# Taking a feed-forward network's two layers in turns on TensorE, product by product, from the seventeenth step on

## The chip, the cores and the metric

One core of a Trainium2 chip. The metric is the device time of one execution in microseconds; lower is better.

## The reference

A chunked attention with memory tokens feeds a squared-ReLU feed-forward network. Cut to what matters:

```python
# attention: 4 batches x 8 heads x 768 positions x 64; chunks of 32 queries,
# each sees 16 positions to the left, 8 to the right and 8 memory tokens (64 keys)
for c in range(nc):
    scores = scale * np.matmul(q_c, k_full.transpose(0, 1, 3, 2))
    scores = scores - np.max(scores, axis=-1, keepdims=True)
    a = np.exp(scores)
    a = a / (np.sum(a, axis=-1, keepdims=True) + 1e-09)
    out[:, :, c_start:c_end] = np.matmul(a, v_full)
x = attn_out.transpose(0, 2, 1, 3).reshape(3072, 512)
h = x @ w_in                      # 512 -> 2048
r = np.maximum(h, 0.0)
g = s * (r * r) + b
return (g @ w_out).astype(np.float32)   # 2048 -> 512
```

## The kernel before, in words

The 3072 tokens are cut into 8 chunks of 384 (`TOK`), the 2048 hidden features into 16 blocks of 128. A **step** `u` is one feature block of one chunk; there are 128 (`STEPS`). Each step has two halves on TensorE:

- `hidden(u)`, the first layer: a 128x384 tile `h` in one PSUM bank, summed over 4 blocks of the 512 inputs. Values are split into a high and a low fp32r part, so each block takes three products (high weight with low x, low weight with high x, high with high). That makes 12 matmuls of 384 columns; the weights stand in the array (`w` or `ww`) and `x` streams.
- `result(u)`, the second layer: three 128x512 accumulators (`acc`, one for each 128 tokens, each with its bank), again three products each: 9 matmuls of 512 columns; here the tile `g` stands in the array and the weights stream.

Each matmul has a weight load of its own, which runs beside the matmul ahead of it. Between the halves of a step ScalarE makes relu, square, `s*x+b` and the high part `gH` out of `h`, all in place in PSUM up to the last, and VectorE makes the low part `gL`. There are three `g` tiles and at most two `h` tiles.

The whole program is laid out ahead of time by `Plan`: every operation is put down with its engine, an assumed duration (`HOLD`), its dependences and a priority. `Plan.lay` then runs through time and gives each free engine the ready operation with the lowest priority number; the instructions are written in that order, and the engines work through their queues in it. `hidden(u)` has priority `u` and is put down in pieces (before: 4 pieces of three products); `result(u)` has priority `u + LAG - 0.1` with `LAG = 2`, in three pieces, one for each accumulator. So in the steady part TensorE takes result(u-1), hidden(u+1), result(u), hidden(u+2) and so on, each whole.

Between these lie, every eight steps, the **attention blocks** of the coming chunks: 96 small matmuls for values (line 502) and 96 for scores (line 481) in one pinned chain, then softmax and 24 32x32 transposes on VectorE (line 440). Until about 126 us VectorE and ScalarE also turn the float64 weights into split parts (lines 588 to 597). Names in the profile: `ps` is any PSUM bank, `xH`/`xL` the parts of x, `w`/`ww` prepared weights, `gH`/`gL` the parts of g. Line 610 is the first layer's matmul, 633 the second's.

Of the kernel before, what the change touches and what calls it, by code (L numbers as in the profile page):

```python
# [21 lines left out]
B, H, S, D = 4, 8, 768, 64  # L22
# [3 lines left out]
P = 128  # L26
# [3 lines left out]
NC_T = DM // P  # L30
NF = DFF // P
TOK = 384
# [10 lines left out]
NTURN = 2  # L43
SECOND = 1.0
LAG = 2
NALONE = 2
JOIN = 2.0
APART = 6.0
# [16 lines left out]
def G_AT(i, a):  # L65
# [11 lines left out]
LATE_F = NF - NEARLY  # L77


HOLD = dict(hidden=523, result=690, scores=560, value1=670, value2=670, scores1=540, scores2=540, turn=84, value=1300, wrest=1000, warm=215,  # L80
            relu=388, square=388, affine=565, high=388, xhigh=388, wscale=566, whigh=527, copy=270, exp8=570, exp4=385, keep=480, store=480,
            low=555, rec=90, edge=90, max8=600, max4=335, sub8=600, sub4=335, sum8=600, sum4=335, flip=317, xlow=500, wlow=350, wjoin=640, wsign=617, out=620,
            small=235, norm8=1040, norm4=560, issue=440)
LATE = dict(PE=185, ACT=135, DVE=140, POOL=60, SP=0)
# [6 lines left out]


class Op:
    __slots__ = ("eng", "hold", "fn", "deps", "outs", "prio", "lock", "vals", "n", "start", "end", "left", "ready", "size", "done", "next")


class Val:
# [37 lines left out]
        self.live[v.kind] -= 1  # L135


class Plan:


# [3 lines left out]
    def op(self, eng, kind, prio, fn, reads=(), writes=(), lock=False, size=0):  # L144
        o = Op()
        o.eng, o.hold, o.fn, o.prio, o.lock, o.n, o.size = eng, HOLD[kind], fn, prio, lock, len(self.ops), size
        o.deps, o.outs, o.vals, o.next = set(), [], [], None
        for part in reads:
            o.deps.update(part[1])
        for part in writes:  # L150
            o.deps.update(part[1])
            o.deps.update(part[2])
        for part in reads:
            part[2].append(o)
        for part in writes:
            part[1][:] = [o]
            part[2].clear()
        o.vals = list({id(p[0]): p[0] for p in (*reads, *writes)}.values())
        for v in o.vals:
            v.left += 1  # L160
        self.ops.append(o)
        return o

    def lay(self, filler=None):

# [18 lines left out]
        while todo:  # L184
            t = heapq.heappop(events)
            while events and events[0] <= t:
                heapq.heappop(events)
            while back and back[0][0] <= t:
                v = heapq.heappop(back)[-1]
                v.ring.back(v)  # L190
            for e in engines:
                while waiting[e] and waiting[e][0][0] <= t:
                    o = heapq.heappop(waiting[e])[2]
                    heapq.heappush(ready[e], (o.prio, o.n, o))
                if free[e] > t:
                    continue
                if e == "SP":
                    flying = [x for x in flying if x > t]
                    if len(flying) >= FLIGHT:
                        heapq.heappush(events, min(flying))  # L200
                        continue
                put, got = [], None

                soon = min(((y[2].prio, y[1], y[0]) for y in waiting[e] if y[0] <= t + SOON[e]), default=None) if SOON[e] else None
                while ready[e]:
                    x = heapq.heappop(ready[e])
                    o = x[2]
                    if soon and soon[:2] < x[:2]:
                        put.append(x)
                        heapq.heappush(events, soon[2])  # L210
                        break
                    if e in pin and pin[e] is not o:
                        put.append(x)
                        continue
                    new = [v for v in o.vals if v.slot is None and v.ring.tiles is not None]
                    other = "POOL" if e == "DVE" else "DVE"
                    held = o.lock and e in lock and lock[other] > t

                    if o.lock and e in lock and free[other] <= t and any(y[2].lock and y[:2] < x[:2] for y in ready[other]):
# [24 lines left out]
                o = got  # L244
                o.start = t
# [5 lines left out]
                if o.size:  # L251
                    wire = max(wire, t) + o.size / (RATE if sent >= NSLOW else SLOW)
                    sent += 1
                    o.end = wire + LAND
                    flying.append(o.end)
                if o.lock and e in lock:
                    lock[e] = free[e]
                laid.append((t, o.n, o.fn))
                todo -= 1
                heapq.heappush(events, free[e])  # L260
                for d in o.outs:
                    d.left -= 1
                    d.ready = max(d.ready, free[e] + AGAIN[e] if d.eng == e and not o.size else o.end)
                    if not d.left:
                        heapq.heappush(waiting[d.eng], (d.ready, d.n, d))
                        heapq.heappush(events, d.ready)
                for v in o.vals:
                    v.left -= 1
                    v.done = max(getattr(v, "done", 0.0), o.end)
                    if not v.left and v.ring.tiles is not None:  # L270
                        heapq.heappush(back, (v.done, o.n, o.vals.index(v), v))
                        heapq.heappush(events, v.done)
# [9 lines left out]
def body(ctx: ExitStack, tc: tile.TileContext, qkv, w1, w2, out):  # L282
    nc = tc.nc
# [120 lines left out]
    def xt(x, a, c):  # L404
        return x.tile[2 * a + c // 2][:, c % 2 * TOK:(c % 2 + 1) * TOK]
# [194 lines left out]

    g_vals, h_vals, a_vals, partial = {}, {}, {}, {}

    def hidden(u):
        ch, f = STEPS[u]
        h = Val(ps, "h")
        x, w = x_vals[ch], c_w[0, f]

        def products(c):
            for n, (wi, xi) in enumerate(((0, 1), (1, 0), (0, 0))):
                nc.tensor.matmul(h.tile[:, :TOK], weight_tile(0, f)[:, wi, c * P:(c + 1) * P], xt(x, xi, c), start=(c == 0 and n == 0),  # L610
                                 stop=(c == NC_T - 1 and n == 2))
# [13 lines left out]
    def result(u):  # L625
# [2 lines left out]
        first = u == 0 or STEPS[u - 1][0] != ch  # L628
        last = u + 1 == len(STEPS) or STEPS[u + 1][0] != ch

        def products(acc, t):
            for n, (gi, wi) in enumerate(((1, 0), (0, 1), (0, 0))):
                nc.tensor.matmul(acc.tile, g.tile[gi][:, t * P:(t + 1) * P], weight_tile(1, f)[:, wi, :], start=(first and n == 0), stop=(last and n == 2))  # L633
# [85 lines left out]
```

## Time and profile before

| | |
|---|---|
| median of 3 runs | 627.71 us (625.8, 627.71, 628.86) |
| the profiled execution's own time | 625.31 us |
| its span, from the first to the last instruction | 623.5 us |
| TensorE busy | 97% of the span |
| VectorE and ScalarE busy | 55% each |
| TensorE's granted clock, mean | 0.996 |

The views that follow are of that profiled execution. A matmul's busy time in them (0.34 us for 384 columns, 0.39 us for 512) includes the tail that the next one overlaps; what a matmul costs in a row of matmuls is the distance from its start to the next one's start.

### The profile page before, as it was taken

To read this page: it belongs to the slowest core of one execution; us is meant where nothing else is said; L and a number is where in the kernel's file an instruction comes from. 1 tells how busy PE (TensorE), PEld (TensorE's weight loads), DVE (VectorE), ACT (ScalarE), POOL (GpSimd) and SP (SyncE) were. 2 spreads that over 40 slices of the span, in tenths; PEclk is the share of its full clock that TensorE was granted. 3 is DMA by queue.
4 is the path that set the end of the run, shared out by engine and by line. 5 is a ranking of instruction groups with operands and counts; after the bars stand their busy time and mean duration, and the time that the engine had idled before them with its cause. 6 is when DMAs were issued, how large, how long until landed. Compare 5 with 4: busy or idle time off the path is not lost.

```text
span 623.5 us, 13759 instructions
## 1 busy us (share of the span) xinstructions
PE 605.3 (97%) x5854; PEld 532.3 (85%) x5861; DVE 341.3 (55%) x816; ACT 343.7 (55%) x660; POOL 37.2 (6%) x46
## 2 busy tenths in 40 slices
PE   8898999999999999999999999999999999999997
PEld 5667888888989898898988899898988989899996
DVE  6899999884565462825538182654618355131112
ACT  3577888854555554454455555545555445545543
POOL 2112000000010000101001010100101000000000
PEclk9899999999999999999999999999999999999999
DMA  9944766413041300303022030312103110010001
GB/s 348 400 159 145 243 188 183 131 50 129 1 128 50 112 18 12 134 34 128 1 82 98 2 128 1 129 50 77 53 2 127 52 53 0 2 50 2 1 0 52
DMA packets 17342, 55.42 MB, mean 89 GB/s; under 512 B 1920, under 2 KB 1920, under 8 KB 17280
## 3 DMA queue, kind: packets, MB, share of 16 engines
q1 hardware_dynamic: 17280, 54.53, 25.4%
q8 instruction: 46, 0.75, 0.5%
q14 instruction: 16, 0.13, 0.1%
HBM read 48.24 MB, written 6.29 MB: 87 GB/s over the span
## 4 chain that ended last, share of the span: by engine, by line
PE 82%; DVE 11%; DMA 4%; issue 2%; ACT 1%; POOL 0%; DVEq 0%; SPq 0%; ACTq 0%
PE ps L610 37%; PE ps L633 37%; DMA words<-w 4%; PE ps L502 3%; PE ps L481 3%; DVE wv L591 2%; DVE wv L593 2%; PE ps L371 1%; DVE top L419 1%; DVE t L420 1%; DVE den L422 1%; DVE gL L622 1%; DVE w L597 1%; DVE ww L597 1%; DVE words L589 1%
## 5 line engine op out<-in xcount | busy, mean ns | idle before, releaser
L622 DVE TENSOR_TENSOR gL<-ps,gH 128x384 fp32r<-128x384 f32 x128 | 70.9, 555 | 232.1 <-ACT gH L621 231.2
L618 ACT ACTIVATE ps<-ps 128x384 f32<-128x384 f32 x128 | 60.8, 475 | 191.5 <-PE ps L610 190.5
L610 PE MATMUL ps<-xH,w 128*128 128x384 f32 x512 | 130.9, 336 | 0.3 <-DVE w L597 0.3
L610 PE MATMUL ps<-xH,ww 128*128 128x384 f32 x512 | 130.7, 336 | 0.0
L633 PE MATMUL ps<-w,gH 128*128 128x512 f32 x384 | 119.1, 391 | 0.0
L633 PE MATMUL ps<-ww,gH 128*128 128x512 f32 x384 | 119.0, 391 | 0.0
L610 PEld LDWEIGHTS ps<-xH,w 128*128 128x128 f32 x512 | 92.7, 188 | 3.0 <-DVE w L597 0.9
L610 PEld LDWEIGHTS ps<-xH,ww 128*128 128x128 f32 x512 | 92.8, 188 | 2.2
L440 DVE STREAM_TRANSPOSE aT<-t 32x128 f32<-32x128 f32 x288 | 86.9, 302 | 7.2 <-POOL t L425 2.7
L610 PE MATMUL ps<-xL,w 128*128 128x384 f32 x256 | 87.4, 341 | 2.0 <-DVE top L419 1.3
L610 PE MATMUL ps<-xL,ww 128*128 128x384 f32 x256 | 86.8, 339 | 0.0
L620 ACT ACTIVATE ps<-ps,b_sb,s_sb 128x384 f32<-128x384 f32 x128 | 82.3, 643 | 4.2
L633 PEld LDWEIGHTS ps<-ww,gH 128*128 128x128 f32 x384 | 72.1, 188 | 13.3
L633 PEld LDWEIGHTS ps<-w,gH 128*128 128x128 f32 x384 | 72.1, 188 | 13.2
L633 PE MATMUL ps<-w,gL 128*128 128x512 f32 x192 | 76.3, 398 | 1.2 <-DVE gL L622 1.0
L633 PE MATMUL ps<-ww,gL 128*128 128x512 f32 x192 | 75.9, 395 | 1.1 <-DVE gL L622 1.1
L621 ACT ACTIVATE gH<-ps 128x384 fp32r<-128x384 f32 x128 | 62.9, 491 | 3.9
L619 ACT ACTIVATE ps<-ps 128x384 f32<-128x384 f32 x128 | 60.8, 475 | 4.0
L425 POOL TENSOR_TENSOR t<-t,rden 96x512 f32<-96x512 f32 (+1 forms) x36 | 34.8, 967 | 471.2 <-DVE rden L424 372.9
L610 PEld LDWEIGHTS ps<-xL,w 128*128 128x128 f32 x256 | 48.0, 187 | 5.4 <-DVE top L419 1.4
L610 PEld LDWEIGHTS ps<-xL,ww 128*128 128x128 f32 x256 | 48.0, 187 | 2.8
L633 PEld LDWEIGHTS ps<-w,gL 128*128 128x128 f32 x192 | 36.0, 187 | 8.7 <-DVE gL L622 2.4
(51 smaller groups left out, 439.9 us busy)
## 6 DMA issues: line engine op xcount, KB each, us to landing
raw<-qkv SPq DMA_DIRECT2D x28, 576.0 KB, 6.0
words<-w SPq DMA_DIRECT2D x24, 512.0 KB, 4.0
v<-qkv SPq DMA_DIRECT2D x28, 384.0 KB, 3.9
out<-partial SPq DMA_DIRECT2D x24, 256.0 KB, 2.1
early<-w SPq DMA_DIRECT2D x8, 512.0 KB, 10.5
early<-qkv SPq DMA_DIRECT2D x3, 576.0 KB, 6.4
early<-qkv SPq DMA_DIRECT2D x4, 384.0 KB, 8.5
early<-qkv SPq DMA_DIRECT2D x1, 577.0 KB, 3.7
```

Of the source, the lines that this page charges most:

```text
L425: op("POOL", "norm" + size, late + 0.25, lambda: nc.gpsimd.tensor_tensor(tv(), tv(), wide(rden), ALU.mult), (st["r", key],), (t[key],), lo ...
L440: nc.vector.transpose(aT.tile[rows, :, c, r * CHUNK:(r + 1) * CHUNK], t.tile[c * CHUNK:(c + 1) * CHUNK, r::2, g * CHUNK:(g + 1) * CHUNK])
L481: nc.tensor.matmul(S[n].tile[c * CHUNK:(c + 1) * CHUNK, (at * GB + j) * CELL:(at * GB + j + 1) * CELL], raw.tile[rows, k * CHUNK:(k + 1) * ...
L502: nc.tensor.matmul(V[p].tile[n * D + e:n * D + e + CHUNK, to:to + 2 * CHUNK], vals_[p].tile[:, at(n) + e:at(n) + e + CHUNK], aT[n].tile[:, ...
L591: op("DVE", "wjoin", due, lambda: nc.vector.scalar_tensor_tensor(bits(), bits(), 3, lo(), ALU.logical_shift_left, ALU.bitwise_or), (raw["l ...
L610: nc.tensor.matmul(h.tile[:, :TOK], weight_tile(0, f)[:, wi, c * P:(c + 1) * P], xt(x, xi, c), start=(c == 0 and n == 0), stop=(c == NC_T ...
L618: op("ACT", "relu", u, lambda: nc.scalar.activation(hp(), hp(), AF.Relu), (), (h[0],))
L619: op("ACT", "square", u, lambda: nc.scalar.activation(hp(), hp(), AF.Square), (), (h[0],))
L620: op("ACT", "affine", u, lambda: nc.scalar.activation(hp(), hp(), AF.Identity, scale=s_sb, bias=b_sb), (c_s[0], c_b[0]), (h[0],))
L621: op("ACT", "high", u, lambda: nc.scalar.activation(g.tile[0], hp(), AF.Copy), (h[0],), (g["H"],))
L622: op("DVE", "low", u, lambda: nc.vector.tensor_tensor(g.tile[1], hp(), g.tile[0].bitcast(F32), ALU.subtract), (h[0], g["H"]), (g["L"],))
L633: nc.tensor.matmul(acc.tile, g.tile[gi][:, t * P:(t + 1) * P], weight_tile(1, f)[:, wi, :], start=(first and n == 0), stop=(last and n == 2))
```

## The change

From step 16 on (`MIX = 16`, so the seventeenth), the pieces of `hidden` and `result` carry a side, "h" or "r", and a list of their single products (`cut`). When the planner picks a piece with a side for TensorE, it looks for the first ready piece of the other side (`mate`), and if there is one, both are laid down as one with their products in alternation (`weave`): the longer list first, so h, r, h, r, h, r, h. The pieces of `hidden` are now three of four products each (assumed 696 ns, before four of three at 523), so that a step's three pieces of either half pair off. This regrouping holds for all steps; a piece now names only the parts of x that its own products read. Durations, priorities and the number of products stay.

```diff
+MIX = 16
-HOLD = dict(hidden=523, result=690, ...
+HOLD = dict(hidden=696, result=690, ...
+def weave(*ops):
+
+    a, b = sorted(ops, key=lambda o: -len(o.cut))
+    for i, fn in enumerate(a.cut):
+        fn()
+        if i < len(b.cut):
+            b.cut[i]()
+    def mate(self, ready, o):
+
+        for x in sorted(ready, key=lambda x: x[:2]):
+            m = x[2]
+            if not m.side or m.side == o.side:
+                continue
+            new = [v for v in m.vals if v.slot is None and v.ring.tiles is not None]
+            if len(new) > 1 or not all(v.ring.can(v) for v in new):
+                return None
+            for v in new:
+                v.ring.give(v)
+            ready.remove(x)
+            heapq.heapify(ready)
+            return m
+        return None
...
-                free[e] = t + o.hold
-                o.end = free[e] + LATE[e]
+                both = [o]
+                if o.side:
+                    mate = self.mate(ready[e], o)
+                    if mate:
+                        both.append(mate)
+                free[e] = t + sum(o.hold for o in both)
+                if len(both) > 1:
+                    laid.append((t, o.n, lambda both=both: weave(*both)))
+                else:
+                    laid.append((t, o.n, o.fn))
...
-        for c in range(NC_T):
-            op("PE", "hidden", u - 0.2 * (u + 1 == len(STEPS)), lambda c=c: products(c),
-               (*(x[a, c // 2, r] for a in "HL" for r in range(2)), w["H"], w["L"]), (h[0],))
+        for k in range(0, 3 * NC_T, NC_T):
+            cs = {j // 6 for j in range(k, k + NC_T)}
+            mix(op("PE", "hidden", u - 0.2 * (u + 1 == len(STEPS)), None,
+                   (*(x[a, d, r] for a in "HL" for d in cs for r in range(2)), w["H"], w["L"]), (h[0],)),
+                u >= MIX and "h", [lambda j=j: product(j) for j in range(k, k + NC_T)])
...
-            op("PE", "result", u + LAG - 0.1, lambda acc=acc, t=t: products(acc, t), (g["H"], g["L"], w["H"], w["L"]), (acc[0],))
+            mix(op("PE", "result", u + LAG - 0.1, None, (g["H"], g["L"], w["H"], w["L"]), (acc[0],)),
+                u >= MIX and "r", [lambda acc=acc, t=t, n=n: product(acc, t, n) for n in range(3)])
```

TensorE's queue in a step far from any attention block, before: here the first layer's tile of feature block 4 (bank `ps_149`), then the second layer for block 3.

```order
L610 MATMUL ps_149<-xL_1_95,w_4_109 128x384
L610 MATMUL ps_149<-xH_1_93,w_4_109 128x384 x2
L610 MATMUL ps_149<-xL_1_95,w_4_109 128x384
L610 MATMUL ps_149<-xH_1_93,w_4_109 128x384 x2
L610 MATMUL ps_149<-xL_1_96,w_4_109 128x384
L610 MATMUL ps_149<-xH_1_94,w_4_109 128x384 x2
L610 MATMUL ps_149<-xL_1_96,w_4_109 128x384
L610 MATMUL ps_149<-xH_1_94,w_4_109 128x384 x2
L633 MATMUL ps_151<-w_3_117,gL_99 128x512
L633 MATMUL ps_151<-w_3_117,gH_98 128x512 x2
```

And from the same step of the changed kernel (its lines 650 and 674 are the old 610 and 633), the first layer of block 4 with the second layer of block 2:

```order
L650 MATMUL ps_153<-xL_0_91,w_4_109 128x384
L674 MATMUL ps_150<-w_2_116,gL_101 128x512
L650 MATMUL ps_153<-xH_0_89,w_4_109 128x384
L674 MATMUL ps_150<-w_2_116,gH_100 128x512
L650 MATMUL ps_153<-xH_0_89,w_4_109 128x384
L674 MATMUL ps_150<-w_2_116,gH_100 128x512
L650 MATMUL ps_153<-xL_0_91,w_4_109 128x384
L650 MATMUL ps_153<-xH_0_89,w_4_109 128x384
L674 MATMUL ps_149<-w_2_116,gL_101 128x512
```

The nine products of the second layer now each lie between two of the first; three times in a step two products of the first layer still follow each other. A step's second layer is that of two steps back.

VectorE's queue after an attention block, before (`t_135`, `t_136` the softmax tiles, `aT` their transposes, `ps_148` and the like the `h` banks that `gL` is made from):

```order
L422 TENSOR_REDUCE den_78<-t_136 96x8
L423 TENSOR_SCALAR den_78<-den_78 96x8
L424 RECIPROCAL rden_79<-den_78 96x8
L440 STREAM_TRANSPOSE aT_139<-t_135 32x4x32 x8
L622 TENSOR_TENSOR gL_101<-ps_148,gH_100 128x384
L440 STREAM_TRANSPOSE aT_139<-t_135 32x4x32 x3
L440 STREAM_TRANSPOSE aT_140<-t_136 32x4x32 x9
L622 TENSOR_TENSOR gL_103<-ps_150,gH_102 128x384
```

The same place in the changed kernel (455, 457 to 459, 475, 663 are the old 420, 422 to 424, 440, 622):

```order
L457 TENSOR_REDUCE den_78<-t_136 96x8
L458 TENSOR_SCALAR den_78<-den_78 96x8
L459 RECIPROCAL rden_79<-den_78 96x8
L475 STREAM_TRANSPOSE aT_139<-t_135 32x4x32 x4
L663 TENSOR_TENSOR gL_101<-ps_152,gH_100 128x384
L475 STREAM_TRANSPOSE aT_139<-t_135 32x4x32 x8
L475 STREAM_TRANSPOSE aT_140<-t_136 32x4x32 x4
L663 TENSOR_TENSOR gL_103<-ps_148,gH_102 128x384
```

Both softmax sums now stand ahead of the first `gL`, with fewer transposes; twelve transposes stand ahead of the second `gL`, as before.

The end of TensorE's queue before (`ww_1432`, `ww_1501`, `ww_1539` belong to the last three feature blocks):

```order
L610 MATMUL ps_147<-xL_1_96,ww_1539 128x384
L610 MATMUL ps_147<-xH_1_94,ww_1539 128x384 x2
L633 MATMUL ps_151<-ww_1432,gL_103 128x512
L633 MATMUL ps_151<-ww_1432,gH_102 128x512 x2
L633 MATMUL ps_154<-ww_1432,gL_103 128x512
L633 MATMUL ps_154<-ww_1432,gH_102 128x512 x2
L633 MATMUL ps_152<-ww_1432,gL_103 128x512
L633 MATMUL ps_152<-ww_1432,gH_102 128x512 x2
L633 MATMUL ps_151<-ww_1501,gL_99 128x512
```

And in the changed kernel (`ww_1438`, `ww_1500`, `ww_1544`):

```order
L650 MATMUL ps_148<-xH_1_94,ww_1544 128x384
L674 MATMUL ps_151<-ww_1438,gH_102 128x512
L650 MATMUL ps_148<-xH_1_94,ww_1544 128x384
L674 MATMUL ps_154<-ww_1500,gL_99 128x512
L674 MATMUL ps_154<-ww_1500,gH_98 128x512 x2
L674 MATMUL ps_150<-ww_1500,gL_99 128x512
L674 MATMUL ps_150<-ww_1500,gH_98 128x512 x2
L674 MATMUL ps_151<-ww_1500,gL_99 128x512
L674 MATMUL ps_151<-ww_1500,gH_98 128x512 x2
L674 MATMUL ps_154<-ww_1544,gL_101 128x512
```

Before, two whole second layers (18 matmuls) lie between the last `h` and the second layer that reads it; now one (9).

## Rows read from the trace of the kernel before

**Rows 1.** The page: busy time by engine, and TensorE's granted clock in 40 slices of the span (tenths of full speed).

```profile
PE 605.3 (97%) x5854; PEld 532.3 (85%) x5861; DVE 341.3 (55%) x816; ACT 343.7 (55%) x660; POOL 37.2 (6%) x46
PEclk9899999999999999999999999999999999999999
```

**Rows 2.** The page: shares of the chain that ended last, by engine and by line.

```profile
PE 82%; DVE 11%; DMA 4%; issue 2%; ACT 1%; POOL 0%; DVEq 0%; SPq 0%; ACTq 0%
PE ps L610 37%; PE ps L633 37%; DMA words<-w 4%; PE ps L502 3%; PE ps L481 3%; DVE wv L591 2%; DVE wv L593 2%; PE ps L371 1%; DVE top L419 1%; DVE t L420 1%; DVE den L422 1%; DVE gL L622 1%; DVE w L597 1%; DVE ww L597 1%; DVE words L589 1%
```

**Rows 3.** Waits of TensorE: first two rows from 128 us to the end, then one of the whole span (line, waited for: us in total, times, longest).

```profile
PE ps L481 <- issue: 4.5, 4, 1.2
PE ps L610 <- DVE top L419: 1.3, 1, 1.3
...
PE ps L633 <- DVE gL L622: 2.1, 4, 1.0
```

**Rows 4.** The chain in order of time, around 345 us, after an attention block and at the end (start us, us, what).

```profile
345.59 2.09 PE ps L610 x12
347.68 2.06 PE ps L633 x9
349.74 2.09 PE ps L610 x12
...
373.36 2.09 PE ps L610 x12
375.45 1.61 PE ps L633 x7
...
609.16 4.19 PE ps L610 x24
613.35 6.14 PE ps L633 x27
```

**Rows 5.** The timeline of a quiet stretch near the end (start us, us, engine, line, operation; x2 means two instructions in a row).

```profile
606.94 0.39 PE L633 MATMUL ps<-ww,gL 128*128 128x512 f32 x1
607.14 0.47 ACT L618 ACTIVATE ps<-ps 128x384 f32<-128x384 f32 x1 [1.97 <-PE ps L610]
...
607.63 0.40 PE L633 MATMUL ps<-ww,gL 128*128 128x512 f32 x1
...
608.32 0.39 PE L633 MATMUL ps<-ww,gL 128*128 128x512 f32 x1
...
609.00 0.34 PE L610 MATMUL ps<-xL,ww 128*128 128x384 f32 x1
...
609.35 0.56 DVE L622 TENSOR_TENSOR gL<-ps,gH 128x384 fp32r<-128x384 f32 x1 [3.60 <-ACT gH L621]
...
615.24 0.39 PE L633 MATMUL ps<-ww,gL 128*128 128x512 f32 x1
...
617.28 0.39 PE L633 MATMUL ps<-ww,gL 128*128 128x512 f32 x1
```

**Rows 6.** The timeline of TensorE at 46.5 us: three second-layer matmuls between small ones and the first layer.

```profile
46.53 0.50 PE L633 MATMUL ps<-w,gL 128*128 128x512 f32 x1
46.88 0.64 PE L633 MATMUL ps<-w,gH 128*128 128x512 f32 x2
47.35 0.33 PE L610 MATMUL ps<-xL,w 128*128 128x384 f32 x1
```

**Rows 7.** The timeline of all engines through an attention block, cut to what is counted: values (line 502) from 357.98 us, the first layer again from 360.61.

```profile
357.98 1.55 PE L502 MATMUL ps<-aT,v 128*32 128x64 f32 x96
358.93 0.49 ACT L516 ACTIVATE xH<-ps 128x384 fp32r<-128x384 f32 x1 [0.72 <-PE ps L502]
359.45 1.23 DVE L517 TENSOR_TENSOR xL<-ps,xH 128x384 fp32r<-128x384 f32 x2 [0.65 <-ACT xH L516]
...
360.61 0.44 PE L610 MATMUL ps<-xL,w 128*128 128x384 f32 x1
...
360.85 0.69 DVE L419 TENSOR_REDUCE top<-ps 96x8 f32<-96x512 f32 x1
...
361.57 0.69 DVE L420 TENSOR_TENSOR t<-ps,top 96x512 f32<-96x512 f32 x1
...
364.95 1.04 POOL L425 TENSOR_TENSOR t<-t,rden 96x512 f32<-96x512 f32 x1 [32.46 <-DVE rden L424]
...
366.26 0.63 DVE L422 TENSOR_REDUCE den<-t 96x8 f32<-96x512 f32 x1
...
369.90 0.56 DVE L622 TENSOR_TENSOR gL<-ps,gH 128x384 fp32r<-128x384 f32 x1
370.49 3.77 DVE L440 STREAM_TRANSPOSE aT<-t 32x128 f32<-32x128 f32 x12
374.29 0.56 DVE L622 TENSOR_TENSOR gL<-ps,gH 128x384 fp32r<-128x384 f32 x1
```

**Rows 8.** The timeline of TensorE in the attention block at 145 us, and the page's row of the queue that brings instructions (packets, MB, share).

```profile
145.30 1.55 PE L502 MATMUL ps<-aT,v 128*32 128x64 f32 x96
146.78 0.95 PE L481 MATMUL ps<-raw 64*32 64x64 f32 x70
148.84 0.52 PE L481 MATMUL ps<-raw 64*32 64x64 f32 x26 [1.11 <-issue]
...
q8 instruction: 46, 0.75, 0.5%
```

More of the change, by code (lines that the diff above doesn't have):

```diff
@@ L77 @@
 LATE_F = NF - NEARLY
-HOLD = dict(hidden=523, result=690, scores=560, value1=670, value2=670, scores1=540, scores2=540, turn=84, value=1300, wrest=1000, warm=215,
+HOLD = dict(hidden=696, result=690, scores=560, value1=670, value2=670, scores1=540, scores2=540, turn=84, value=1300, wrest=1000, warm=215,
             relu=388, square=388, affine=565, high=388, xhigh=388, wscale=566, whigh=527, copy=270, exp8=570, exp4=385, keep=480, store=480,
@@ L93 @@
 class Op:
-    __slots__ = ("eng", "hold", "fn", "deps", "outs", "prio", "lock", "vals", "n", "start", "end", "left", "ready", "size", "done", "next")
+    __slots__ = ("eng", "hold", "fn", "deps", "outs", "prio", "lock", "vals", "n", "start", "end", "left", "ready", "size", "done", "next", "side", "cut")
 class Val:
@@ L146, in op @@
         o.eng, o.hold, o.fn, o.prio, o.lock, o.n, o.size = eng, HOLD[kind], fn, prio, lock, len(self.ops), size
-        o.deps, o.outs, o.vals, o.next = set(), [], [], None
+        o.deps, o.outs, o.vals, o.next, o.side, o.cut = set(), [], [], None, None, None
         for part in reads:
@@ L244, in lay @@
                 o = got
-                o.start = t
                 pin.pop(e, None)
@@ L248, in lay @@
                     pin[e] = o.next
-                free[e] = t + o.hold
-                o.end = free[e] + LATE[e]
[L251 to L259, printed above, removed]
-                heapq.heappush(events, free[e])
@@ L261, in lay @@
[L261 to L272, printed above, removed]
+                both = [o]
@@ new lines, in lay @@
+                if o.side:
[7 more added lines that the diff above has]
+                    laid.append((t, o.n, o.fn))
+                heapq.heappush(events, free[e])
+                for o in both:
+                    o.start = t
+                    o.end = free[e] + LATE[e]
+                    if o.size:
+                        wire = max(wire, t) + o.size / (RATE if sent >= NSLOW else SLOW)
+                        sent += 1
+                        o.end = wire + LAND
+                        flying.append(o.end)
+                    if o.lock and e in lock:
+                        lock[e] = free[e]
+                    todo -= 1
+                    for d in o.outs:
+                        d.left -= 1
+                        d.ready = max(d.ready, free[e] + AGAIN[e] if d.eng == e and not o.size else o.end)
+                        if not d.left:
+                            heapq.heappush(waiting[d.eng], (d.ready, d.n, d))
+                            heapq.heappush(events, d.ready)
+                    for v in o.vals:
+                        v.left -= 1
+                        v.done = max(getattr(v, "done", 0.0), o.end)
+                        if not v.left and v.ring.tiles is not None:
+                            heapq.heappush(back, (v.done, o.n, o.vals.index(v), v))
+                            heapq.heappush(events, v.done)
@@ L601, in body, with mix @@
     g_vals, h_vals, a_vals, partial = {}, {}, {}, {}
+    def mix(o, side, cut):
+        o.side, o.cut = side or None, cut
+        o.fn = lambda: [fn() for fn in cut]
     def hidden(u):
@@ L606, in hidden, with product @@
         x, w = x_vals[ch], c_w[0, f]
[L608 to L611, printed above, removed]
-        for c in range(NC_T):
-            op("PE", "hidden", u - 0.2 * (u + 1 == len(STEPS)), lambda c=c: products(c),
-               (*(x[a, c // 2, r] for a in "HL" for r in range(2)), w["H"], w["L"]), (h[0],))
+        def product(k):
+            c, n = divmod(k, 3)
+            wi, xi = ((0, 1), (1, 0), (0, 0))[n]
+            nc.tensor.matmul(h.tile[:, :TOK], weight_tile(0, f)[:, wi, c * P:(c + 1) * P], xt(x, xi, c), start=k == 0, stop=k == 3 * NC_T - 1)
+        for k in range(0, 3 * NC_T, NC_T):
[3 more added lines that the diff above has]
+                u >= MIX and "h", [lambda j=j: product(j) for j in range(k, k + NC_T)])
         g = g_vals[u] = Val(gs)
@@ L629, in result, with product @@
         last = u + 1 == len(STEPS) or STEPS[u + 1][0] != ch
-        def products(acc, t):
-            for n, (gi, wi) in enumerate(((1, 0), (0, 1), (0, 0))):
-                nc.tensor.matmul(acc.tile, g.tile[gi][:, t * P:(t + 1) * P], weight_tile(1, f)[:, wi, :], start=(first and n == 0), stop=(last and n == 2))
+        def product(acc, t, n):
+            gi, wi = ((1, 0), (0, 1), (0, 0))[n]
+            nc.tensor.matmul(acc.tile, g.tile[gi][:, t * P:(t + 1) * P], weight_tile(1, f)[:, wi, :], start=(first and n == 0), stop=(last and n == 2))
         for t in range(NT):
```

## The prediction

> **What bounds the kernel now.** I read the page first: TensorE is busy 97% of the span, at full clock but for one slice [rows 1]. Then the shares of the chain that ended last: TensorE has 82% of it, 37% each for the two lines that the change rewrites [rows 2]. So the time is a count of matmuls times the distance from one start to the next, plus what TensorE waits. The waits are few: from 128 us to the end 5.8 us in all, none of it for `g`; over the whole span 2.1 us for `gL`, so before 128 us [rows 3]. A change of the order can act in two ways only: on that distance, or by new waits.
>
> **The distance, from the rows.** A step lasts from 345.59 to 349.74, that is 4.15 us: 2.09 for the twelve products of the first layer, 2.06 for the nine of the second [rows 4]. Per product that is about 0.175 and 0.229. The question is what a product costs when the other layer's product follows it, and the trace before has this at each change of layer, two a step.
>
> - *A first-layer product ahead of a second-layer one.* The only run of 24 first-layer products takes 4.19 us, one of 12 takes 2.09 [rows 4]. Twelve more inside a run cost 2.10, 0.175 each. In a run of 12, eleven are followed by their own kind and the last by the other layer: 2.09 - 11 x 0.175 = 0.165 for that last one. The rows are rounded to 0.01 us, so this is 0.15 to 0.18; I take 0.168, a little short of a run's 0.175.
> - *A second-layer product ahead of a first-layer one.* In a normal run the nine fall into threes (606.94, 607.63, 608.32, 609.00): 0.69, 0.69, 0.68. The last three, whose last product is followed by the first layer, are no dearer. Late in the run of 27 at the end, three threes take 2.04 (615.24 to 617.28), 0.227 each [rows 5]. So a second-layer product costs 0.227 once its run is settled, 0.230 in the first threes just after a change of layer. Woven, every one comes just after a change and just before one; I take 0.228. The dear end is a run of only three at 46.53: from the second to the following first-layer product, 46.88 to 47.35, two distances make 0.47, so 0.235 each [rows 6].
>
> **The change, part by part.**
>
> 1. *Weaving.* By the order, 330 pairs of pieces are woven, 110 steps' worth; each step has nine first-layer products ahead of a second-layer one, nine the other way round, and three first-layer products followed by their own kind. That makes 9 x 0.168 + 9 x 0.228 + 3 x 0.175 = 4.089 us against 4.155 (12 x 0.1745 + 9 x 0.229): 0.066 less, times 110 = **-7.3 us**. By the bounds: with 0.165 and 0.227 a step is 4.053 (-11.2 us); with 0.175 and 0.235 it is 4.215 (+6.6 us).
> 2. *The chain of `g`.* Before, a step's second layer began one whole step after its `h` was complete, and it still does: `h` of the woven step u is complete at the step's end, and result(u) starts with step u+2. From the end of `h` (606.94) relu starts 0.20 later and `gL` ends at 609.91, so 2.97 us [rows 5], against a step of 4.09. The cover shrinks from 1.18 to 1.12 us and still holds in the quiet steps: 0.
> 3. *The last `g`.* Here the cover is gone. Before, 18 second-layer products (4.1 us) lay between the last `h` and its reader; now nine, 9 x 0.227 = 2.04. The chain of 2.97 and some 0.05 for the signal make TensorE wait: **+1.0 us**.
> 4. *After an attention block* VectorE's queue is the place where `gL` could be late. I worked it through with the durations of rows 7, from the start of the values as 0. The first layer returns at 2.63 as before; woven steps then end at about 6.82, 10.91 and 15.00. ScalarE now does relu and square first, so the two `xL` end at 2.84 (before, 359.45 + 1.23 is 2.70); first maximum 3.64, `gL` 4.21; difference, maximum, difference 6.41; the two sums with their reciprocals 7.44 and 8.5; POOL's normalization 8.62; four transposes 9.9; `gL` 10.5, read from 10.91 on. Then twelve transposes (3.77) to 14.3 and `gL` to 14.86, read from 15.00 on. Before, that second `gL` ended at 374.85, and its reader began at about 375.29 (the chain's rows begin some 0.16 after the matmul, as 609.16 against 609.00 [rows 4, 5]), a margin of 0.44 [rows 4, 7]; now 0.14. It holds, barely. Three output copies at the end of a chunk go into the same queue, now between transposes. I take **+0.5 us** over the eleven blocks; 0.3 us late in each would be 3.3.
> 5. *The start of weaving* falls into the time in which VectorE still prepares weights, where all 2.1 us of waits for `gL` lie [rows 3]. The cover there is the same step of 4.1 us: **+0.5**, bounds 0 to the 2.1 once more.
> 6. *Pieces of four products instead of three, before step 16.* The same products in the same bank, one hold of 696 for one of 523; where the first layer has to let something pass, it does so at other points. 0, with 1 us either way.
> 7. *Waits on nothing that the profile shows.* In the block at 145 us TensorE stands still for 1.11 us in the middle of the scores, after 70 of their matmuls; after 128 us such waits come four times, 4.5 us [rows 3, 8]. Instructions arrive in pieces (46 packets of 0.75 MB in all, so 16 KB each [rows 8]), and a block of small matmuls uses them fastest; my guess is that a block stalls if a piece ends at the wrong place in it. The number of TensorE's instructions hardly changes, but each block moves by some twenty of them in the stream, so the count may become three or six: 0, with 2.5 us either way.
>
> The sum: -7.3 + 1.0 + 0.5 + 0.5 = **-5.3 us**. On the profiled execution's own 625.31 that is 620.0. Its time is 2.4 below the median of the runs, 627.71, on which it would be 622.4; I say 621.5, about 1% under the median. What a measurement of this kernel can tell from no change is about 0.5%, 3.1 us.
>
> **The rule that speaks against it.** The distances depend on what follows by 5 to 10 ns in 175 to 230, as the runs of 12 and 24 and the threes show [rows 4, 5]. The Trainium skill ("TensorE: Matmul & The Clock Gate", section "Back-to-back issue gap") gives the distance as columns / 2.4 + 2.5 ns, a function of the columns alone, so 162.5 and 215.8 ns here. By that rule the order of products cannot matter and weaving saves 0. The trace lies 12 to 13 ns above the rule in both layers, so something beside the columns does count, but it shows the saving only at the two changes of layer in a step.
>
> **Rivals.**
>
> - *The order does not matter.* What looks like 0.165 at a change of layer is an earlier start that the next product pays back: the threes right after a change are 0.69 against 0.68 [rows 5], which speaks for it; that a full run of nine ends at 0.68 speaks against. Then weaving gives 0, and 1.0 + 0.5 + 0.5 remain: 627.3 on its own time, about 628.5. This is also the time by the rule above.
> - *Each change of layer costs.* A second-layer product never gets out of the slow start of its run and costs 0.235, as at 46.88 [rows 6], and a first-layer one stays at 0.175: +6.6 + 2.0, so 633.9 on its own time, about 635. It decides for slower from a pair (one of each layer) of 0.409 on, where a run has 0.404: 9 x 0.005 x 110 is 5 us, which with 2 of waits is above 3.1. Against it: the run at 46 us follows small matmuls and not the first layer.
> - *`gL` late after each block.* To make the kernel slower by 3.1 us in spite of weaving, each of eleven blocks would have to wait 0.85 us. The margin of 0.14 speaks for some wait, the working in part 4 against so much.
> - *Better than forecast:* 0.165 and 0.227 hold and the waits are 1 us: -10.2, about 616.5.
>
> **How the numbers follow.** The forecast 0.50, the order does not matter 0.25, each change costs 0.10, `gL` late 0.05, better 0.10. The range takes in the first two and the better one with their bounds for instructions and blocks: 615.5 to 630; what lies above 630 (each change costs, late `gL`) and below holds less than 0.2. Faster by over 0.5%: the better case and most of the forecast (its waits could take 2 us more), with a little of the second, 0.56. Within 0.5%: the second and the rest of the forecast, 0.31. Slower: 0.13. The forecast alone lies between 618 and 625.
>
> **What would show it.** In the profile after: woven steps of 4.09 us (4.05 to 4.22 by the bounds; 4.15 would be the first rival); a wait of TensorE for `gL` of about 1 us ahead of its last nine matmuls; waits for `gL` elsewhere of less than 1 us after 128 us; `issue` waits still near 4.5. I am wrong if the step is not shorter, or if `gL` shows up among the waits with more than 3 us.

## The result and the profile after

The changed kernel takes 630.92 us, median of 11 runs (629.63 to 634.99), against 628.04 for the kernel before, run beside it (11 runs, 625.8 to 628.94). The ratio is 1.0057, 95% interval [1.0036, 1.0078]: slower by 0.57%, where 1% faster was forecast. The profiled execution took 629.65 us with a span of 627.6; before, 625.31 and 623.5.

The page of the changed kernel: TensorE's busy time and granted clock, then the shares of the chain that ended last.

```profile
PE 607.3 (97%) x5851; PEld 534.0 (85%) x5859; DVE 343.9 (55%) x816; ACT 342.4 (55%) x660; POOL 37.2 (6%) x46
...
PEclk9999999999999999999999999999999999999999
...
PE 83%; DVE 10%; issue 3%; ACT 3%; DMA 1%; POOL 0%; DVEq 0%; ACTq 0%; SPq 0%
```

TensorE is still the bound, as in [rows 2], at full clock in every slice ([rows 1] have one slice below it). Its waits of the changed kernel: the first two rows from 128 us to the end, the last two of the whole span (line, waited for: us in total, times, longest).

```profile
PE ps L516 <- issue: 6.3, 5, 1.4
PE ps L674 <- DVE gL L663: 0.8, 1, 0.8
...
PE ps L516 <- issue: 8.6, 7, 1.6
PE ps L674 <- DVE gL L663: 3.2, 6, 1.4
```

Against [rows 3] no large new wait has come: one for `gL` (the last `g`), and five on `issue` with 6.3 us where four with 4.5 and the one of 1.3 for VectorE's maximum stood. The loss is in the distance between products. TensorE's timeline in a quiet stretch near the end (start us, busy us, engine, line, operation):

```profile
604.39 0.39 PE L674 MATMUL ps<-ww,gL 128*128 128x512 f32 x1
604.62 0.34 PE L650 MATMUL ps<-xL,ww 128*128 128x384 f32 x1
604.80 0.39 PE L674 MATMUL ps<-ww,gH 128*128 128x512 f32 x1
605.03 0.34 PE L650 MATMUL ps<-xH,ww 128*128 128x384 f32 x1
605.21 0.40 PE L674 MATMUL ps<-ww,gH 128*128 128x512 f32 x1
605.45 0.33 PE L650 MATMUL ps<-xH,ww 128*128 128x384 f32 x1
605.62 0.34 PE L650 MATMUL ps<-xL,ww 128*128 128x384 f32 x1
605.79 0.39 PE L674 MATMUL ps<-ww,gL 128*128 128x512 f32 x1
```

Seven products, from one `gL` to the next, take 1.40 us, and a step is three of these: 4.20 us, where [rows 4] have 4.15. With the start times in nanoseconds, nearly all quiet steps are 4153 or 4154 before, and from step 22 on all but one are exactly 4200 after (that one 4198). Over some 110 of them, 0.0467 us each is 5.1 us. The cleanest stretch for comparing is that between the attention blocks that start at 174.43 and 503.53 us before, 175.22 and 507.42 after: 72 steps, three `issue` waits in each kernel, 3.11 us longer now, 0.043 a step. Over the whole span, counted at equal work (so many products of the two layers begun), the changed kernel is 1.4 to 1.9 us ahead where the weaving begins, between 113 and 116 us, and 4.1 behind at the last product: some 5.5 to 6 us lost, which are the 5.1 of the steps and the 0.8 of the last `g`. The lead at the start is not the weaving's, and where it comes from is open: two executions of one kernel, that of the first experiment, are 0.3 ahead and 0.15 behind at that place.

### The profile page after: what moved, and what is told of

The parts are those of the page before. It is cut to its first block, busy times and chain, and to the rows that moved or that the text cites. A ratio compares the mean times of both kernels' runs of the same rounds, so it can differ in the third digit from the quotient of the medians.

```text
span 627.6 us, 13755 instructions
## 1 busy us (share of the span) xinstructions
PE 607.3 (97%) x5851; PEld 534.0 (85%) x5859; DVE 343.9 (55%) x816; ACT 342.4 (55%) x660; POOL 37.2 (6%) x46
## 4 chain that ended last, share of the span: by engine, by line
PE 83%; DVE 10%; issue 3%; ACT 3%; DMA 1%; POOL 0%; DVEq 0%; ACTq 0%; SPq 0%
PE ps L650 38%; PE ps L674 37%; PE ps L537 3%; PE ps L516 3%; DVE wv L626 2%; PE ps L406 2%; DMA words<-w 1%; DVE wv L628 1%; DVE gL L663 1%; DVE ww L632 1%; DVE top L454 1%; DVE w L632 1%; DVE words L624 1%; DVE t L455 1%; ACT wv L623 1%
## 5 line engine op out<-in xcount | busy, mean ns | idle before, releaser
L650 PE MATMUL ps<-xH,ww 128*128 128x384 f32 x512 | 159.4, 337 | 0.0
L650 PE MATMUL ps<-xH,w 128*128 128x384 f32 x512 | 157.0, 338 | 0.7 <-DVE w L632 0.7
L674 PE MATMUL ps<-ww,gH 128*128 128x512 f32 x384 | 148.6, 395 | 0.0
L674 PE MATMUL ps<-w,gH 128*128 128x512 f32 x384 | 145.9, 395 | 0.5 <-DVE w L632 0.5
L650 PEld LDWEIGHTS ps<-xH,w 128*128 128x128 f32 x512 | 95.3, 188 | 6.5 <-DVE w L632 1.0
L650 PEld LDWEIGHTS ps<-xH,ww 128*128 128x128 f32 x512 | 95.7, 188 | 5.9
L456 ACT ACTIVATE t<-t 96x512 f32<-96x512 f32 (+1 forms) x36 | 20.9, 582 | 43.2 <-DVE t L455 43.2
```

What stands on the lines that cost most here:

```text
L456: op("ACT", "exp" + size, late + 0.2, lambda: nc.scalar.activation(tv(), tv(), AF.Exp, scale=SCALE), (), (t[key],))
```

## The experiments

A matmul of the first layer is called h here, one of the second r. Steps are lengths of quiet ones, away from attention blocks and the first of a chunk. Each kernel is the changed one with the edit shown. Most were executed once. A step's length repeats to 1 ns within one execution, so one execution tells steps apart where it could not tell total times apart.

**Is it the weaving, or the regrouping?**

```diff
-MIX = 16
+MIX = 1000
```

> The changed kernel with the weaving switched off (pieces of four products stay). Every theory expects the steps of the kernel before, 4.15 us, and a span within 1.5 us of 623.5 apart from waits on nothing that the profile shows. If the regrouping itself were to blame, the span would be near the changed kernel's 627.6.

It took 625.19 us. The chain in order of time near its end (start us, us, what):

```profile
600.38 2.09 PE ps L650 x12
602.47 2.06 PE ps L674 x9
604.53 2.09 PE ps L650 x12
606.62 2.06 PE ps L674 x9
```

From 600.38 to 604.53 is 4.15 us, the step of before, with the same 2.09 and 2.06 as [rows 4]. The loss in the step is the weaving's. The same kernel was later timed:

> The same kernel as in the first experiment: the changed kernel with the weaving off (no step reaches MIX), the first layer still in three pieces of four. If the weaving alone makes the loss, the time is that of the kernel before, ratio 0.998 to 1.002. If the regrouping, or the places that the planner now gives the small operations, cost part of it, the ratio lies above 1.002; the changed kernel itself is at 1.0057.

625.83 us, median of 11 runs (623.52 to 627.97), ratio to before 0.9969, interval [0.9951, 0.9987]. The regrouping costs nothing. That it came out under both expectations, by 0.3%, is not explained: the two profiled executions of this kernel have spans of 623.1 and 623.7 us, before's has 623.5. Set against this kernel, the weaving costs 1.0057 / 0.9969 = 1.0088, some 5.5 us, which is the 5.1 us of the steps and the 0.8 of the last `g`. Against before it is faster, if by little. The one execution of the bank experiment below, at 623.9, lies within its range.

**How does the loss grow with the changes of layer?** Before has two changes of layer in a step, the changed kernel 18. The coarse weaving takes whole pieces in turns, hhhh rrr, six changes:

```diff
-    for i, fn in enumerate(a.cut):
+    for fn in a.cut + b.cut:
         fn()
-        if i < len(b.cut):
-            b.cut[i]()
```

> Pieces are paired as in the changed kernel, but a pair is laid as four products of the first layer and then three of the second: 6 changes of layer in a step in place of 18 (woven) or 2 (before). If every change of layer costs the same, on the line through 4.155 (2 changes) and 4.200 (18), a step takes 4.166 us. If what costs is the slow start of a second-layer run (its first five products, some 12 ns a change before), a step takes 4.19 to 4.21, as much as woven.

625.9 us. Its chain, the first pieces of three steps in a row:

```profile
154.68 0.70 PE ps L648 x4
...
158.84 0.70 PE ps L648 x4
...
163.00 0.70 PE ps L648 x4
```

4.16 us a step. That speaks against the slow start of a second-layer run as the cause (4.19 to 4.21 expected) and lies 0.006 under a fixed price for each change. Already here the h ahead of an r takes 174 ns, and the 168 of before's run of twelve does not come back. Then twelve changes, h h r r h h r:

```diff
-    for i, fn in enumerate(a.cut):
-        fn()
-        if i < len(b.cut):
-            b.cut[i]()
+    for i in range(0, len(a.cut), 2):
+        for fn in a.cut[i:i + 2] + b.cut[i:i + 2]:
+            fn()
```

> Weaving by pairs: within each joined piece h h r r h h r instead of h r h r h r h. That is 12 changes of layer in a step, between the 6 of the coarse weaving (4.160 us a step) and the 18 of the change (4.200). Theory A (a fixed price for each change of layer: 0.0029 us for each of the 16 more than before's two, from 4.154 to 4.200): 4.183 us. Theory B (a step locks into a pattern that a count of changes does not give): another length, most likely one of those already seen, 4.160, 4.20 or 4.24, and the same in all quiet steps.

627.4 us. The `gL` matmuls in two stretches of TensorE's timeline, the first and the fourth of four (three to a step):

```profile
445.96 0.40 PE L673 MATMUL ps<-w,gL 128*128 128x512 f32 x1
...
450.14 0.40 PE L673 MATMUL ps<-ww,gL 128*128 128x512 f32 x1
...
513.65 0.39 PE L673 MATMUL ps<-w,gL 128*128 128x512 f32 x1
...
517.81 0.39 PE L673 MATMUL ps<-w,gL 128*128 128x512 f32 x1
```

The first stretch has 4.18 us a step, the second 4.16. In nanoseconds nearly all quiet steps from 22 on are 4160 or 4180, and the one gives way to the other only at an attention block. So neither expectation is quite right: the price for each change misses the 4.160 that most steps have, and the steps do not all agree. Twelve changes cost little more than six.

**Is it the change of PSUM bank?** Here the weaving is off, and from step 64 on the nine r go round the three accumulators instead of three to each:

```diff
-MIX = 16
+MIX = 1000
+SPREAD = 64
...
+            if u >= SPREAD and not last:
...
+                    o.fn = lambda cuts=cuts: [c[n]() for n in range(3) for c in cuts]
```

> No weaving; from step 64 on the nine products of the second layer go to their three accumulators in turn, so that each writes another PSUM bank than the one before it, as woven products do, with the same streams and loads. If the change of the bank costs, a step goes from 4.15 to about 4.18 to 4.20 at step 64; if not, it stays at 4.15.

623.9 us, and 4.153 us in nearly all quiet steps with either order of the accumulators. Its chain in the stretch that goes round:

```profile
435.38 2.09 PE ps L651 x12
437.47 2.06 PE ps L675 x9
439.53 2.09 PE ps L651 x12
441.62 2.06 PE ps L675 x9
```

Nine r with a change of bank after each take the 2.06 us of [rows 4]. The distances by place in the run (230, 236, 228, 233, 231, 227, 227, 227, 226 ns) are also those of before. A change of bank between two r costs nothing here.

**Is it the place of the operands in memory?** The kernel puts every tile at a chosen offset within 256 bytes. Four settings of these offsets were tried, each with the steps before 64 whole and those from 64 on woven. First, the first layer's weights go from 128 to 192, the place of the second layer's, and `g` from 192 to 128; `x` stays at 64:

```diff
-MIX = 16
+MIX = 64
-    return 192 if half else 128
+    return 192
...
-    return 192
+    return 128
...
-        lo = half * (2 * DM + 16)
+        lo = half * 2 * DM
```

> Weaving from step 64 on, and the operands laid at other places within 256 bytes: first-layer weights at 192, second-layer weights at 192, g at 128, x at 64 as before. So the pairs that stand side by side when woven (x streams while g is loaded, second-layer weights stream while first-layer weights are loaded) get the offsets that the pairs of the unwoven order had, and the other way round. If the places decide, the two stretches swap: steps of 4.20 before step 64 and 4.13 to 4.16 behind it. If the change of layer itself costs, they stay: 4.15 before, 4.20 behind.

627.44 us; whole steps 4.176 and 4.184 in turns, 4.180 on average, woven 4.180: the woven ones 0.020 shorter than in the changed kernel, the whole ones 0.027 longer, and the order no longer matters, though two widths still alternate. Second, tiles spread over all four places:

```diff
-    return 192 if half else 128
+    return 64 * ((f // 4 + half) % 4 if half else f // 2 % 4)
...
-    return 64
+    return 64 * ((2 * a + c + i) % 4)
...
-    return 192
+    return 64 * ((i + a) % 4)
...
```

> Weaving from step 64 on, as in the phase run, but every tile of x, g and the weights lies at a place of its own within 256 bytes (0, 64, 128 or 192, by chunk, part and feature block), so that one trace holds all pairs of streamed and loaded operand, unwoven and woven. If the places decide, the distance of a first-layer product spreads by more than 5 ns between pairs with the same neighbours, and some woven steps come to 4.13 or less. If the change of layer itself costs, the spread is below 3 ns and all woven steps take 4.18 to 4.20.

628.74 us; the steps are no longer alike (4.15 to 4.21), on average about 4.185 whole and 4.182 woven. None comes to the 4.13 that places alone were expected to reach. What each combination of places costs a product is not shown. Third, both streams at 128 and both weight loads at 192:

```diff
-    return 192 if half else 128
+    return 128 if half else 192
...
-    return 64
+    return 128
...
-        lo = half * (2 * DM + 16)
+        lo = (1 - half) * (2 * DM + 16)
```

> Weaving from step 64 on; both streamed operands (x, second-layer weights) start at 128 of 256 bytes and both loaded operands (first-layer weights, g) at 192, so that a change of layer no longer changes a place. Theory of the changing place: a woven step, 4.200 in the changed kernel, falls by what the two parts gained alone (0.039 with the streams from one tile, 0.014 with the loads from one tile), to 4.13 to 4.16, and the unwoven steps gain too, 4.13 to 4.15. Theory of the changing width: the woven step stays at 4.16 to 4.20, since 384 and 512 columns still alternate. Theory of the layer change as such: 4.20.

630.95 us; whole steps 4.178 and 4.189 in turns. The woven ones have two lengths. TensorE's timeline again, the first and the fourth of four `gL` in either stretch:

```profile
450.37 0.39 PE L674 MATMUL ps<-ww,gL 128*128 128x512 f32 x1
...
454.55 0.39 PE L674 MATMUL ps<-ww,gL 128*128 128x512 f32 x1
...
488.03 0.39 PE L674 MATMUL ps<-w,gL 128*128 128x512 f32 x1
...
492.23 0.39 PE L674 MATMUL ps<-w,gL 128*128 128x512 f32 x1
```

4.18 us in the first stretch, 4.20 in the second, with the same order and the same places. In nanoseconds it is 4180 in the quiet steps from 66 to 94 and 4200 from 96 to 126; between them lies an attention block in which TensorE stood still for 1.1 us. Such a stop is not needed: the twelve-change kernel changes between 4160 and 4180 at its blocks at 212 and 248 us, which have none. Fourth, everything at 192:

```diff
-    return 192 if half else 128
+    return 192
...
-    return 64
+    return 192
...
-        lo = half * (2 * DM + 16)
+        lo = half * 2 * DM
```

> As the run before, with all four operands at 192. If only the change from one product to the next counts, the result is that of the run with two places (both 4.13 to 4.16 woven). If the pair of streamed and loaded place counts as well, the two runs differ, in the unwoven stretch too.

634.13 us; whole 4.187, woven 4.240, the longest of all (TensorE's timeline, the first and the fourth of four `gL`):

```profile
498.27 0.39 PE L674 MATMUL ps<-w,gL 128*128 128x512 f32 x1
...
502.51 0.39 PE L674 MATMUL ps<-w,gL 128*128 128x512 f32 x1
```

That products lose time because their places differ from one to the next falls with this: here none differs. Of the five settings the kernel's own is the only one with whole steps of 4.153; the woven ones lie between 4.180 and 4.240. So the loss by weaving depends on the places: 0.047 at the kernel's own, 0 at the first setting, 0.053 with everything at 192.

**Which property of the other layer's product matters?** The second layer's products were made like the first's in one respect at a time, woven here and whole in the next (`MIX = 1000`). In these two and the one after them part of the result is left out or replaced.

```diff
-MIX = 16
+MIX = 48
...
-            nc.tensor.matmul(acc.tile, g.tile[gi][:, t * P:(t + 1) * P], weight_tile(1, f)[:, wi, :], start=...
+            wide = TOK if 64 <= u < 80 and n else DM
+            lhs = weight_tile(0, f)[:, gi, t * P:(t + 1) * P] if 80 <= u < 96 else g.tile[gi][:, t * P:(t + 1) * P]
+            rhs = x_vals[ch].tile[2 * wi][:, :DM] if 96 <= u < 112 else weight_tile(1, f)[:, wi, :]
+            nc.tensor.matmul(acc.tile[:, :wide], lhs, rhs[:, :wide], start=...
```

> Woven from step 48 on, places as in the changed kernel, and in each of three chunks the second layer has one property of the first (so part of the result is not the reference's): steps 64 to 79 stream only 384 columns in two of three products; steps 80 to 95 load their stationary operand from the first layer's weights; steps 96 to 111 stream from x. Woven pairs (one product of each layer) take 0.4095 us in the changed kernel, 0.401 for settled runs. If the change of width costs, the excess of some 9 ns goes in the first stretch (pair of two 384-column products 0.348 to 0.350); if the change of the loaded tile, in the second (0.401); if the change of the streamed tile, in the third (0.401). If none of them, the excess stays in all three.

> The control to the woven run with parts: the same three stretches (part of the result again not the reference's), no weaving. Every theory expects 0.227 to 0.230 for a second-layer product of 512 columns in the stretches with another loaded or streamed tile, and 0.174 to 0.176 for one of 384 columns; what differs from that is the cost of the place of the operand, not of weaving.

625.4 and 621.22 us. Woven, the normal steps are 4.200 (a few at the seams 4.180 or 4.160), those with six of nine r at 384 columns 3.846 to 3.854, those with first-layer weights in the array 4.187, those with x streaming 4.160. The narrow stretch, woven (timeline, one `gL` for each third of a step):

```profile
348.81 0.40 PE L677 MATMUL ps<-w,gL 128*128 128x512 f32 x1
350.09 0.39 PE L677 MATMUL ps<-w,gL 128*128 128x512 f32 x1
351.38 0.40 PE L677 MATMUL ps<-w,gL 128*128 128x512 f32 x1
352.66 0.39 PE L677 MATMUL ps<-w,gL 128*128 128x512 f32 x1
```

and whole (chain):

```profile
347.73 2.09 PE ps L650 x12
349.83 1.75 PE ps L677 x9
351.58 2.09 PE ps L650 x12
```

3.85 us by both: with most widths equal the loss is gone. With first-layer weights in the array the woven step is the longer, 4.187 against 4.164 to 4.169 whole. With x streaming in both layers it is the shorter. Woven (timeline, the first and the fourth of four `gL`), then whole (chain, first layer alone):

```profile
491.41 0.40 PE L677 MATMUL ps<-xH,gL 128*128 128x512 f32 x1
...
495.57 0.40 PE L677 MATMUL ps<-xH,gL 128*128 128x512 f32 x1
```

```profile
490.63 2.10 PE ps L650 x12
...
494.81 2.10 PE ps L650 x12
```

4.16 us woven against 4.18 whole, with the widths of 384 and 512 still in alternation. So two widths in alternation do not make the loss by themselves; what streams and the places decide as well. The last experiment takes the width alone to its end, with four stretches in one kernel:

```diff
-MIX = 16
+MIX = 48
...
+            wide = TOK if 64 <= u < 96 and not (first and n == 0) else DM
...
-                u >= MIX and "h", ...
+                (MIX <= u < 80 or u >= 112) and "h", ...
```

> The weaving is on in steps 16 to 79 (from 48 on in this kernel) and again from step 112, off in steps 80 to 111. In steps 64 to 95 every product of the second layer but a chunk's first ones streams 384 columns instead of 512, so the last quarter of those results is left out. So there are four stretches: woven and normal, woven and all 384 wide, whole and all 384 wide, whole and normal. Theory A (the loss comes where products of two widths follow each other): 21 products of about 0.1745 make 3.66 us a step, and the woven and the whole stretch agree within 0.01. Theory B (the loss comes where the kind of operand changes, whatever the width): the woven stretch stays 0.04 to 0.05 above the whole one, 3.70 to 3.71. In the normal stretches 4.20 woven and 4.15 to 4.18 whole, by both.

Woven with all 384 wide (timeline, `gL` alone), then whole with all 384 wide (chain, first layer alone):

```profile
348.28 0.34 PE L675 MATMUL ps<-w,gL 128*128 128x384 f32 x1
349.50 0.34 PE L675 MATMUL ps<-w,gL 128*128 128x384 f32 x1
350.72 0.34 PE L675 MATMUL ps<-w,gL 128*128 128x384 f32 x1
351.94 0.34 PE L675 MATMUL ps<-w,gL 128*128 128x384 f32 x1
```

```profile
409.43 2.10 PE ps L650 x12
...
413.09 2.09 PE ps L650 x12
...
416.74 2.09 PE ps L650 x12
```

3.66 us woven; 3.65 or 3.66 whole (in nanoseconds 3660 and 3653). The normal stretches of the same kernel have 4200 and 4153. So at the kernel's own places 0.007 of the 0.047 us are left when all products are 384 wide: some 85% of this loss goes with the wide products. Whether it needs the alternation of two widths or only the 512 columns is not settled, since no run has all products at 512.

## Why the prediction was wrong

**Part 1, the weaving, is the step that failed.** It read the price of a product followed by the other layer off the two changes of layer in a step: 0.168 for h, 0.228 for r. The readings were right (in nanoseconds, the last h of before's run takes 168 and the last r 226), but they are prices of the last place in a run of twelve and of nine. With runs of four the h ahead of an r already takes 174. Woven, the h ahead of an r take 0.176, 0.181 and 0.175, the one ahead of an h 0.171, and the r 0.229, 0.231 and 0.237 in turns: 9 x 0.1773 + 3 x 0.171 + 9 x 0.2323 = 4.200. Of the 0.111 us by which the step exceeds the forecast 4.089, the h ahead of an r make 0.084 and the r 0.039, and the h ahead of an h take 0.012 off. The term is +5.1 us where the text has -7.3, though inside its bounds (4.053 to 4.215), near the dear end. The first rival's doubt, an early start that is paid back, fits before's run: the last h takes 168, but the first two r behind it take 230 and 236 against 226 at its end. The second rival, "each change of layer costs", had the right direction: it decides from a pair of 0.409 on, and a pair is 0.410. Its reason, a second-layer product that never leaves the slow start of its run, fits the r of 0.229 to 0.237, but it has no dearer h, where most of the miss lies; the coarse weaving, with every r near the start of a run, takes 4.160 all the same, and the twelve-change kernel fits no fixed price for each change.

**What stands in its place.** The distance does not belong to a product and its successor. A step settles into a repeating pattern: 4.153 before and 4.200 after, 4.160, 4.176 to 4.189 and 4.240 in the experiments. Which one depends on the order, on the widths that alternate and on the operands' places, and, by the two lengths in one kernel, on how the run starts. What in TensorE makes these patterns was not found. The Trainium skill ("TensorE: Matmul & The Clock Gate", section "Back-to-back issue gap") gives columns / 2.4 + 2.5 ns, a function of the columns alone, for a matmul by itself; of a stream of weight loads and matmuls, as here, it says that both set the spacing, which the prediction leaves out. The trace lies above the formula, and the order and the places count: the same products take 4.153 to 4.240 us a step. With all products 384 wide the order hardly counts (3.653 against 3.660), but a product still takes 0.174 us, where the formula has 0.1625.

**The other parts.**

- Part 2 held: after 128 us the only wait for `gL` is that of the last `g`.
- Part 3 held: 0.8 us, forecast 1.0.
- Part 4, +0.5 at the blocks: no wait for `gL` stands behind one. The margin of 0.14 us that it worked out for a step of 4.09 is wider with one of 4.20.
- Part 5: ahead of 128 us `gL` makes 3.2 - 0.8 = 2.4 us against the 2.1 of [rows 3]: +0.3, forecast +0.5. That the numbers are near is luck: from 100 to 128 us, where the weaving starts, `gL` makes 0.6 against 1.1 before, and the growth lies at 60 to 100 us, ahead of the first woven products at 114 us.
- Part 6: the regrouping costs nothing. Timed, it even gains 1.8 us (0.8 to 3.1 by the interval), where 0 was taken with 1 us either way; why is open.
- Part 7, waits on `issue`: after 128 us 6.3 us in five, against 4.5 in four. The fifth of before is the wait put down to VectorE's maximum in the block at 503 us (1.28 us): that maximum ended at 507.06, TensorE began at 507.49, in the changed kernel the same block has an `issue` wait of 1.2, and by its place in the stream of instructions it is one of them (see the last section). So it is 5.8 against 6.3, +0.5 where 0 was taken with 2.5 either way.

## What to carry to other kernels

A price that a trace shows at one place in a run of matmuls is not the price of that neighbourhood: ahead of reordering hundreds of them, run a stretch in the new order. Here the new length was there within a few steps, and one profile shows it to the nanosecond, though it can change at the next interruption. In a kernel whose operands are placed so that the present order suits them, a new order can lose that: whole runs were worth 0.047 us a step at this kernel's own places and nothing at another setting, so the places have to be tried anew for a new order. When a change does two things, time each alone: here one of them is harmless, or even a small gain, and the other is the loss.

## What the runs showed that was not expected

- The same order at the same places ran at exactly 4180 ns a step up to one attention block and at exactly 4200 from the next on; the twelve-change weaving went between 4160 and 4180 in the same way. These are fixed lengths and no noise.
- Nearly all settled lengths are whole multiples of 6.67 ns (20/3) over the period in which they repeat. Whole steps of 4153.3, 4180 and 4186.7 ns are 623, 627 and 628 of these, those of 3653.3 are 548; the thirds of woven steps (1386.7, 1393.3, 1400, 1413.3 and, all 384 wide, 1220 ns) are 208, 209, 210, 212 and 183. So a step does not lengthen by a little for each dearer product: it goes from one such length to another. What sets this unit no run shows.
- Operand offsets within 256 bytes moved a step by up to 0.03 us whole and 0.06 woven, with the same instructions in the same order: whole steps 4.153 to 4.187 on average, woven 4.180 to 4.240.
- Where an attention block stalls depends on where it lies in the stream of instructions. TensorE at the first block after 128 us in the changed kernel, and the page's row of the queue that brings instructions:

```profile
145.59 1.55 PE L537 MATMUL ps<-aT,v 128*32 128x64 f32 x96
147.07 0.82 PE L516 MATMUL ps<-raw 64*32 64x64 f32 x59
149.26 0.63 PE L516 MATMUL ps<-raw 64*32 64x64 f32 x37 [1.38 <-issue]
...
q8 instruction: 46, 0.75, 0.5%
```

  The packets are as many as in [rows 8], but the stop comes after 59 scores instead of 70 and takes 1.38 us instead of 1.11, and the block at 322 us, free before, has one now, while that at 247 us has lost its own. The guess in part 7, a piece of instructions that ends at the wrong place in a block, has more for it. TensorE's weight loads and matmuls number 11732 in the trace of before, 255 for each of the 46 packets. Counted among them, its five stops after 128 us stand at 3259, 5307, 6075, 9659 and 10427 (the last is the wait put down to VectorE), all 187 above a multiple of 256; the five of the changed kernel all stand 186 above one. In each of the twelve experiments, too, all stops of more than 0.9 us in the blocks stand at one place between multiples of 256. Every block holds at least one such place and only four to six of them stop; which ones do is not explained.
